# Attention and a two-layer network on one core: first weight kept in its loaded row order, heads renumbered, prologue reordered by unit of the hidden layer

## The chip, the core and the metric

The kernel runs on one core of a Trainium2 chip. The metric is device time in microseconds (us), from three timed runs; a profiled execution gives the time of every instruction. The core's engines run side by side, each in the order of its own instructions, and wait for each other by semaphores: TensorE (PE, matmuls; PEld are its weight loads), VectorE (DVE), ScalarE (ACT), GpSimd (POOL) and SyncE (SP, which here issues most DMAs). A matmul keeps one operand in the array (the weights, loaded beforehand, up to 128 x 128) and streams the other one, up to 512 columns. Results go to PSUM, eight banks of 512 float32 a partition; ACT and DVE move them to SBUF.

## The reference

There are B = 8 batches of H = 8 heads; a head has S = 512 rows of D = 64, and a state of NS = 32 rows. Each reads the other by softmax attention; the results, with heads side by side, are 544 rows of 512 a batch, and go through a layer norm and two weight matrices with a ReLU and a residual. The weights come as float64.

```python
scores = scale * x @ state.T                       # 512 x 32 a head
a = softmax(scores);   xread = a @ state           # 512 x 64
scores2 = scale * state @ x.T                      # 32 x 512
a2 = softmax(scores2); sread = a2 @ x              # 32 x 64
x = concat([xread, sread], rows), heads side by side   # 544 x 512 a batch
xn = (x - mean) / sqrt(var + 1e-6) * g_ln
out = x + relu(xn @ w_ch1) @ w_ch2                 # 512 x 2048, 2048 x 512
```

## The kernel before

The kernel keeps float32 accuracy with float16 matmuls: a value is split in a high and a low half, and a product is three matmuls (`TERMS`: high by high, high by low, low by high). As xread is a @ state, the first layer is a @ (state @ w1): **state products** (`state_products`, L662) multiply the states by w1 once a batch into `matrix`, and first products multiply `matrix` by the numerators `ea`. The hidden layer of 2048 is worked in U = 4 units of 512.

**Streams and the order.** Each function is a generator that yields single steps (one instruction, or a group of matmuls). `streams` (L930) lists them all, and `PLAN` (L40) is a written-out order: "17:3" issues step 3 of stream 17. `issue` (L191) only follows it, so each engine works off its steps in this order and waits where an operand or buffer isn't ready. `WARM` (L163) is the count of matmuls over constants, without use for the result, that the order puts between others.

**Prologue.** `attention(0)` (L346) works with `parts = 2`: 256 rows at a time. It finds the largest magnitudes, splits x and state (`x16`, `sh`), transposes them by DMA (`xT`, `sT`), takes scores (`scores`, L402), and softmax both ways. `weights1(u)` (L583) loads two halves of 1 MB of w1, makes float32 words of the float64 (`words`, L567: one ACT and two DVE instructions a half), subtracts the mean with matmuls in float32 (`means`, L599, and four DVE instructions), and finds a scale: ACT writes magnitudes, four matmuls over `ones` add them (`add`, L608), DVE takes the largest. Then `split` writes high and low halves, and four DMAs (L623) copy them into `w1c`, in which each 64-row head lies as high beside low. A state product is thus two passes over 128 rows, (high, high) and (low, low) of the state against (high, low) of the weight, for two groups of four heads: in each, four heads at once in column strips of 32:

```python
for a in range(2):
    for j in range(4):
        nc.tensor.matmul(ps[32 * j:32 * j + 32], lhsT=sT[:, g, a, 32 * j:32 * j + 32],
                         rhs=w[:, 2 * g + j // 2, j % 2], start=a == 0, stop=a == 1, ...)
```

`weights2(u)` (L625) does w2 alike; its scale comes from ACT with an accumulated sum and `across` (L324: a transpose, a reduction, a broadcast by matmul, a maximum). In the order before, all four `weights1` come first, then the state and first products of batch 0, then `weights2` and `second_products_by_unit` (L721). Sums and differences of w2's blocks (`sums_of_weights`, L743) serve the later batches' products with seven instead of eight block products. `common_scale` (L652) needs all units.

**A later batch.** `products(b)` (L774) runs, for two halves of the rows and four units, first products (L801), ReLU and sums on ACT, DVE and POOL, and 42 second products (L857); meanwhile the order has `attention(b + 1)` and `state_products(b + 1)` issued between them. There the state products take their results from the two PSUM banks `half`, which the first products use too, and scores, reads and mixes use the pair `banks` (a ring of one). **State reads** (`read_state`, L477): for each head and each quarter of the rows one matmul, with high and low half of x side by side as 128 weight columns and 64 columns streamed; ACT copies the result `z`, and `fold_halves` (L491) adds high and low with four float32 matmuls. Four small DMAs collect the reads of all batches in `sread_rows`; `state_rows` (L900) normalizes these 256 rows, and `products(8)` takes them through both layers (`first_of_state`, L806), with a copy of the weight's high halves in order of rows (`high_halves`, L893, eight DMAs).

## Time and profile before

| | |
|---|---|
| Timed runs | 666.25 us median of 3 (665.38 to 669.15) |
| Profiled execution, first to last instruction | 665.1 us |
| PE busy | 643.9 us in 6051 matmuls |
| DVE busy | 499.5 us in 1002 instructions |
| ACT busy | 388.8 us in 699 |
| POOL busy | 217.9 us in 189 |
| HBM read, written | 28.05 MB, 9.44 MB |
| Issue to landing of a 1 MB weight load | 8.2 to 8.6 us (median) |

The profile names an instruction by its line, engine, operation and "out<-in" with the program's tile names. Steps that go through `do` have the line of that helper, L188; matmul groups have the line of the matmul. A matmul's duration includes its way through the array, so matmuls that follow each other overlap; the distance from start to start shows what each costs in a stream. A tile shape such as 128*32 gives rows and columns of the weights.

### The profile page before, as it was taken

The page shows a single profiled execution, that of the slowest core. Times are in us where ns is not written, and L with a number is a line of the kernel's source. Part 1 is how long each engine was busy: PE and PEld are TensorE (multiplying, and loading weights), DVE is VectorE, ACT ScalarE, POOL GpSimd, SP SyncE. Part 2 cuts the span into 40 slices and gives each one's busy share as a digit, 9 for nine tenths or more (in the row PEclk, how much of TensorE's full clock was granted, in tenths as well). Part 3 has the DMA queues.
Part 4 walks back from the last instruction along what each step waited for, and adds up shares of the span by engine and source line. Part 5 has one row for each costly group of instructions (what it writes and reads, how often), then busy time and mean ns, then how long its engine had stood idle before and what let it go on. Part 6 is the DMA issues. An engine that isn't in the chain of part 4 may idle for free.

```text
span 665.1 us, 14886 instructions
## 1 busy us (share of the span) xinstructions
PE 643.9 (97%) x6051; PEld 499.6 (75%) x6051; DVE 499.5 (75%) x1002; ACT 388.8 (58%) x699; POOL 217.9 (33%) x189
## 2 busy tenths in 40 slices
PE   7997999999999999999999999999999999999996
PEld 2343655549887887788888888888778887888885
DVE  5998976687788677967887689777976897465533
ACT  5498889667546474547465656465546564344331
POOL 0000443321344315323452226333433343234222
PEclk8999999999999999999999999999999999999999
DMA  8999846825131434340416152405142411245211
GB/s 323 309 276 209 257 130 132 138 57 135 43 67 43 130 105 78 96 100 2 92 33 163 67 88 68 100 2 121 38 125 46 77 33 42 82 116 98 78 57 32
DMA packets 98564, 69.64 MB, mean 105 GB/s; under 512 B 72704, under 2 KB 90624, under 8 KB 98048
## 3 DMA queue, kind: packets, MB, share of 16 engines
q1 hardware_dynamic: 96384, 64.77, 38.4%
q0 software_dynamic: 864, 3.15, 2.5%
q8 instruction: 47, 0.77, 0.5%
q10 hardware_dynamic: 1248, 0.79, 0.4%
q14 instruction: 21, 0.17, 0.1%
HBM read 28.05 MB, written 9.44 MB: 56 GB/s over the span
## 4 chain that ended last, share of the span: by engine, by line
PE 86%; DVE 8%; DMA 3%; ACT 1%; issue 1%; SPq 0%; DVEq 0%
PE acc L857 41%; PE half L801 22%; PE acc L717 6%; PE half L667 5%; PE half L810 3%; DVE w_t L188 2%; PE acc L703 2%; PE acc L749 2%; PE banks L481 1%; PE banks L405 1%; PE banks L517 1%; DMA w1c<-raw 1%; DMA raw<-in_moe_w_ch_dram 1%; PE banks L494 1%; DMA x_f<-in_x_dram 1%
## 5 line engine op out<-in xcount | busy, mean ns | idle before, releaser
L857 PEld LDWEIGHTS <-xs 128*128 128x128 f16 x2520 | 242.4, 98 | 43.6 <-issue 15.3
L188 POOL TENSOR_TENSOR xs<-rs,xs 128x512 f16<-128x512 f32 x120 | 142.5, 1200 | 272.6 <-ACT xs L188 207.1
L857 PE MATMUL acc<-w2h,xs 128*128 128x256 f16 x1440 | 183.0, 273 | 0.0
L801 PE MATMUL half<-ea,matrix 128*128 128x256 f16 x1344 | 159.4, 273 | 0.0
L801 PEld LDWEIGHTS <-matrix 128*128 128x128 f16 x1344 | 130.7, 98 | 16.7 <-issue 0.8
L857 PE MATMUL acc<-sums,xs 128*128 128x256 f16 x1080 | 141.9, 273 | 0.0
L188 DVE SCALAR_TENSOR_TENSOR rs<-half,rs 128x256 f32<-128x256 f32 x224 | 89.4, 419 | 27.6 <-ACT rs L188 13.3
L188 ACT ACTIVATE xs<-rs 128x512 f16<-128x512 f32 x128 | 77.1, 618 | 40.5 <-DVE rs L188 33.8
L188 ACT ACTIVATE xs<-half 128x256 f16<-128x256 f32 (+1 forms) x112 | 53.7, 487 | 73.2 <-PE half L801 51.3
L188 DVE SCALAR_TENSOR_TENSOR xs<-half,xs 128x256 f16<-128x256 f32 (+1 forms) x112 | 61.2, 550 | 28.1 <-ACT xs L188 24.5
L188 ACT ACTIVATE matrix<-half,hs 128x512 f16<-128x512 f32 x56 | 38.1, 687 | 35.2 <-PE half L667 34.9
L188 DVE SCALAR_TENSOR_TENSOR matrix<-half,hs,matrix 128x512 f16<-128x512 f32 x56 | 41.2, 742 | 16.0 <-ACT matrix L188 15.3
L188 ACT ACTIVATE rs<-half 128x256 f32<-128x256 f32 x56 | 21.4, 382 | 42.4 <-PE half L801 40.0
L717 PE MATMUL acc<-w2h,hid 128*128 128x512 f16 x192 | 43.1, 379 | 0.0
L188 DVE TENSOR_TENSOR strip<-acc,strip 128x256 f32<-128x256 f32 (+1 forms) x60 | 33.2, 554 | 10.5 <-PE acc L857 7.5
L667 PE MATMUL half<-w1c,sT 128*32 128x512 f16 x448 | 33.5, 384 | 1.9 <-DVE rs L188 1.0
L717 PEld LDWEIGHTS <-hid 128*128 128x128 f16 x192 | 18.5, 98 | 20.9 <-issue 0.4
L188 POOL TENSOR_TENSOR ts<-ts,mA 128x1024 f32<-128x1024 f32 (+1 forms) x8 | 14.4, 1806 | 59.3 <-DVE mA L188 52.9
L188 PE MATMUL half<-ones 128*128 128x512 bf16 x103 | 28.0, 416 | 1.1 <-DVE ones L309 1.1
L188 DVE SCALAR_TENSOR_TENSOR x<-x_f,x_s,x 128x512 f16<-128x512 f32 x32 | 24.8, 799 | 5.3 <-ACT x L188 5.3
L188 POOL TENSOR_TENSOR hid<-strip,hid 128x512 f16<-128x512 f32 x16 | 19.5, 1232 | 26.9 <-ACT hid L188 26.8
L188 DVE BATCH_NORM_STATS2 s<-xr 128x6 f32<-128x512 f32 x32 | 21.6, 684 | 8.7 <-ACT xr L188 8.6
(154 smaller groups left out, 791.5 us busy)
## 6 DMA issues: line engine op xcount, KB each, us to landing
raw<-in_moe_w_ch_dram SPq DMA_DIRECT2D x9, 1024.0 KB, 8.6
out_dram<-xr SPq DMA_DIRECT2D x16, 512.0 KB, 3.7
x_f<-in_x_dram SPq DMA_DIRECT2D x15, 512.0 KB, 5.0
sums<-in_moe_w_ch_dram SPq DMA_DIRECT2D x7, 1024.0 KB, 8.2
ek<-ea SPq DMA_DIRECT2D x56, 64.0 KB, 2.0
ek<-ek SPq DMA_DIRECT2D x7, 512.0 KB, 4.3
xr<-part POOLq DMA_DIRECT2D x6, 512.0 KB, 5.0
w1c<-raw SPq DMA_DIRECT2D x8, 256.0 KB, 6.8
```

Of the source, the lines that this page charges most:

```text
L188: return lambda: f(*map(now, args), **{k: now(v) for k, v in kw.items()})
L405: nc.tensor.matmul(o[32 * j:32 * j + 32], lhsT=sT[:, g, a, 32 * j:32 * j + 32], rhs=xT[:, s, 4 * g + j].rearrange("p c t -> p (c t)"), sta ...
L481: nc.tensor.matmul(ps_z[:, h // 4, :, h % 4], lhsT=xv[:, c // hc, h, c % hc], rhs=ebT[:, :, h // 4, c, 32 * (h % 4):32 * (h % 4) + 32], st ...
L494: nc.tensor.matmul(pr[:, g], lhsT=z4[:, g, i], rhs=fold, start=i == 0, stop=i == 1, skip_group_check=True)
L517: nc.tensor.matmul(px[:, c, D * h:D * h + D], lhsT=ek[:, h // 4, h % 4, (2 * t + c) * P:(2 * t + c + 1) * P], rhs=sk[:, h], start=True, st ...
L667: nc.tensor.matmul(ps[32 * j:32 * j + 32], lhsT=sT[:, g, a, 32 * j:32 * j + 32], rhs=w[:, 2 * g + j // 2, j % 2], start=a == 0, stop=a == ...
L703: nc.tensor.matmul(o[:, 256 * f:256 * f + 256], lhsT=m[:, g, i, P * (q + f):P * (q + f) + P], rhs=ea[:, s, k, g], start=f == 0 and g == 0 ...
L717: nc.tensor.matmul(po, lhsT=hid[:, i, q, c * P:(c + 1) * P], rhs=w[:, j, q], start=first and q == 0 and n == 0, stop=last and q == 3 and n ...
L749: nc.tensor.matmul(o, lhsT=signs[:, k // 2], rhs=v[k], start=start and k == 0, stop=k == 3, skip_group_check=True)
L801: nc.tensor.matmul(ps[:, 256 * q:256 * q + 256], lhsT=m[:, h, i, P * (2 * k + q):P * (2 * k + q) + P], rhs=ea[:, 0, j, h, 256 * g:256 * g ...
L810: nc.tensor.matmul(ps[:, 256 * q:256 * q + 256].rearrange("p (t n) -> p t n", t=2), lhsT=w[:, k // 2, k % 2, fs] if k < H else wn[:, k - H ...
L857: nc.tensor.matmul(po[o], lhsT=y[:, n, i, o] if o < 2 else x[:, o - 2, n, i], rhs=v[j], start=u == 0 and n == 0 and k == 0 and o in (2, 1, ...
```

## The change

- `w1c` is no longer copied: `weights1` splits straight into it in the order of rows as loaded, with high and low halves as two blocks. Row d of an odd head lies in the upper 64 partitions. Head h = 2j + g goes to strip j of group g, where it was h = 4g + j; `state_of` finds its state, and batch 0 loads its state so.
- State products: three passes by `TERMS` over 64 rows each, both groups (row halves) and four heads (column strips) in one step of 24 matmuls. In batches from 1 on they write both banks of `banks`, and one ACT and one DVE instruction take both out.
- Scales: PE multiplies the upper 16 bits of the float32 words by themselves (`largest_square`: 16 matmuls of 128 x 128 a unit and weight), DVE takes the largest element, `across` follows, and the scale comes from its square root's exponent. The Abs passes and sums over `ones` go.
- State reads: 64 weight columns a matmul, two heads in two column strips, three of the four half products; DVE adds high and low, one PE transpose replaces `fold_halves`.
- Words are made in place (`t = raws[0]`), with other buffers.
- The streams of the prologue stand by unit: first weight, state products, first products, second weight, second products. The order (`PLAN`) is new throughout; `WARM` is 55, was 103. In the new order no warming matmul stands ahead of the first weight's `means`.
- The last stage uses the same weights without `high_halves`; its row transposes have eight blocks, had twelve.

```diff
+        if b > 0:
+            yield do(nc.sync.dma_start, out=sj, in_=state[b].rearrange("(g j) n d -> (j n) g d", g=G))
+        else:
+            for j in range(4):
+                yield do(nc.scalar.dma_start, out=sj[32 * j:32 * j + 32],
+                         in_=state[b, 2 * j:2 * j + 2].rearrange("g n d -> n g d"))
...
+    def scales_of_squares(m, s, inv, c):
+
+        yield do(nc.vector.tensor_scalar, inv.bitcast(I32), m.bitcast(I32), 1, HALF_EXP_MASK, ALU.logical_shift_right,
+                 ALU.bitwise_and)
+        yield do(nc.vector.tensor_scalar, inv, inv, 2.0**64 / c, None, ALU.mult)
+        yield do(nc.vector.reciprocal, s, inv)
...
+    def state_of(b, sT, g, j, a):
+
+        k, i = ((2 * j + g) // 4, (2 * j + g) % 4) if b > 0 else (g, j)
+        return sT[:, k, a, 32 * i:32 * i + 32]
...
-            for h in range(H):
+            for j in range(4):
                 for c in range(C):
-                    nc.tensor.matmul(ps_z[:, h // 4, :, h % 4], lhsT=xv[:, c // hc, h, c % hc],
-                                     rhs=ebT[:, :, h // 4, c, 32 * (h % 4):32 * (h % 4) + 32],
-                                     start=c == 0, stop=c == C - 1, skip_group_check=True)
+                    for i in range(2):
+                        for g in range(G):
+                            nc.tensor.matmul(ps_z[64 * g:64 * g + 64, j, 0:2 - i], lhsT=xv[:, c // hc, 2 * j + g, c % hc, i],
+                                             rhs=ebT[:, 0:2 - i, g, c, 32 * j:32 * j + 32],
+                                             start=c == 0 and i == 0, stop=c == C - 1, skip_group_check=True)
...
-        yield do(nc.scalar.activation, z, pz[:, 0], AF.Copy)
-
-        def fold_halves(pr, z4):
...
-        yield do(fold_halves, pr, z4)
+        yield do(nc.vector.tensor_reduce, z.rearrange("p (j n) -> p j n", j=4), ps_z.rearrange("p j i n -> p j n i"), AX.X,
+                 ALU.add)
+        yield do(nc.tensor.transpose, pz[:, 1, 0:P], z, idf)
...
+    def largest_square(t, total, m, top, col):
+
+        tops = t.bitcast(BF16).rearrange("p (e two) -> p e two", two=2)
+
+        def gram(v, ps, first, last):
+            for k in range(8):
+                c = v[:, 128 * k:128 * k + 128, 1]
+                nc.tensor.matmul(ps, lhsT=c, rhs=c, start=first and k == 0, stop=last and k == 7)
+        for h in range(2):
+            yield do(gram, tops[:, 1024 * h:1024 * h + 1024], total[:, 0:P], h == 0, h == 1)
+        yield do(nc.vector.tensor_reduce, col, total[:, 0:P], AX.X, ALU.max)
+        yield from across(col, 1, 1, m, top, total[:, P:3 * P])
...
+        yield from largest_square(t, accumulator(), m, of_weights[:, u, 3:4], of_weights[:, u, 1:2])
+        yield from scales_of_squares(m, scale, is1[:, u:u + 1], SW)
+        yield from split(w[:, 0], w[:, 1], t, scale)
+        w1c[u] = w.rearrange("p i (j f) -> p i j f", j=4)
...
+        def multiply(ps, sT, w):
+            for n, (i, k) in enumerate(TERMS):
                 for j in range(4):
-                    nc.tensor.matmul(ps[32 * j:32 * j + 32], lhsT=sT[:, g, a, 32 * j:32 * j + 32],
-                                     rhs=w[:, 2 * g + j // 2, j % 2], start=a == 0, stop=a == 1, skip_group_check=True)
+                    for g in range(G):
+                        r = slice(64 * g, 64 * g + 64)
+                        nc.tensor.matmul(ps[g][32 * j:32 * j + 32], lhsT=state_of(b, sT, g, j, i)[r], rhs=w[r, k, j],
+                                         start=n == 0, stop=n == 2, skip_group_check=True)
...
+                ps = banks()
+                scale = hs[:, u:u + 1]
+                yield do(lambda p, *a: multiply([p[:, g] for g in range(G)], *a), ps, sT, w1c[u])
+                yield do(nc.scalar.activation, m[:, :, 0], ps, AF.Copy, scale=scale)
+                yield do(nc.vector.scalar_tensor_tensor, m[:, :, 1], ps, scale, m[:, :, 0], ALU.mult, ALU.subtract)
...
-    streams = [gain(), attention(0), *map(weights1, range(U)), state_products(0), first_products(), *map(weights2, range(U)),
-               common_scale(), *map(second_products_by_unit, range(U)), attention(1), state_products(1),
-               *map(sums_of_weights, range(U))]
+    streams = [gain(), attention(0)]
+    for u in range(U):
+        streams += [weights1(u), state_products(0, (u,)), first_products(u), weights2(u), second_products_by_unit(u)]
+    streams += [common_scale(), attention(1), state_products(1), *map(sums_of_weights, range(U))]
```

More of the change, by code (lines that the diff above doesn't have):

```diff
@@ L30 @@
 S2 = 2.0**12
-CM = 2.0**-20
-SB = 2.0**15
+CM = 2.0**-24
+SB = 2.0**19
 SR = 2.0**-6
@@ L291, in load_batch @@
             yield do(engines[hh].dma_start, out=xf[:, hs], in_=src[:, hs])
-        yield do(nc.sync.dma_start, out=sj, in_=state[b].rearrange("(g j) n d -> (j n) g d", g=G))
+        if b > 0:
[4 more added lines that the diff above has]
+                         in_=state[b, 2 * j:2 * j + 2].rearrange("g n d -> n g d"))
         for r in range(4 if b > 0 else 0):
@@ L604, in weights1 @@
             yield do(nc.vector.scalar_tensor_tensor, t4[:, k], t4[:, k], gx[:, k:k + 1], ps, ALU.mult, ALU.subtract)
-        sizes = raws[0].bitcast(BF16)[:, 0:2048]
-        yield do(nc.scalar.activation, sizes, t, AF.Abs)
-        def add(total, v):
-            for k in range(4):
-                nc.tensor.matmul(total, lhsT=ones, rhs=v[:, 512 * k:512 * k + 512], start=k == 0, stop=k == 3)
-        yield do(add, total, sizes)
-        yield do(nc.vector.tensor_reduce, m, total, AX.X, ALU.max)
-        yield do(nc.vector.tensor_scalar_max, m, m, TINY)
-        yield from scales(m, scale, is1[:, u:u + 1])
-        hl = raws[1].bitcast(F16).rearrange("p (i e) -> p i e", i=2)
-        yield from split(hl[:, 0], hl[:, 1], t, scale)
-        hl = hl.rearrange("p i (k f) -> p i k f", k=4)
-        w = narrow(u, "w1c").bitcast(F16).rearrange("p (k s f) -> p k s f", k=4, s=2)
-        w1c[u] = w
-        for i in range(2):
-            for s in range(2):
-                to = 64 * (i ^ s)
-                yield do(nc.sync.dma_start, out=w[to:to + 64, :, s], in_=hl[64 * s:64 * s + 64, i])
+        yield from largest_square(t, accumulator(), m, of_weights[:, u, 3:4], of_weights[:, u, 1:2])
+        yield from scales_of_squares(m, scale, is1[:, u:u + 1], SW)
+        yield from split(w[:, 0], w[:, 1], t, scale)
+        w1c[u] = w.rearrange("p i (j f) -> p i j f", j=4)
     def weights2(u):
@@ L820, in block @@
                         else:
-                            yield do(first_of_state, ps, k, w1c[u], high[u], state_rows_T[0])
+                            yield do(first_of_state, ps, k, w1c[u], state_rows_T[0])
                             r = rs[:, 512 * k:512 * k + 512]
@@ L889, in products @@
             yield together()
-    high, state_rows_T = [None] * U, [None]
-    def high_halves(u):
-        high[u] = quad("high").bitcast(F16).rearrange("p (k f) -> p k f", k=4)
-        for s in range(2):
-            half = slice(64 * s, 64 * s + 64)
-            yield do(nc.sync.dma_start, out=high[u][half], in_=w1c[u][half, :, s])
+    state_rows_T = [None]
     def state_rows():
@@ L939, in moe_attention @@
         streams += these
-    streams += [list(state_rows()), *(list(high_halves(u)) for u in range(U))]
+    streams.append(list(state_rows()))
     streams += [list(s) for s in products(B)]
```

162 lines of the change are left out of this document (78 added, 84 removed), and 243 rows, old and new, of the table PLAN.

## The prediction

> **What bounds the kernel now.** I read the page first, for the busy shares and the chain.
>
> ```profile
> span 665.1 us, 14886 instructions
> PE 643.9 (97%) x6051; PEld 499.6 (75%) x6051; DVE 499.5 (75%) x1002; ACT 388.8 (58%) x699; POOL 217.9 (33%) x189
> PE 86%; DVE 8%; DMA 3%; ACT 1%; issue 1%; SPq 0%; DVEq 0%
> ```
>
> TensorE carries the chain. The table by stretches says where it does not. Its columns are length, then busy time and count of PE, PEld, DVE, ACT, POOL, then granted clock, DMA share and GB/s.
>
> ```profile
> 0.00:16.00 16.00, 11.42 (x36) 4.26 (x36) 8.86 (x23) 8.83 (x15) 0.70 (x6) 0.89 0.88 320
> 16.00:42.00 26.00, 23.37 (x111) 9.90 (x112) 25.64 (x46) 16.37 (x17) 0.00 (x0) 1.00 1.06 314
> 42.00:64.00 22.00, 17.67 (x185) 9.10 (x185) 19.93 (x29) 18.43 (x26) 2.10 (x2) 1.00 0.98 219
> 64.00:82.00 18.00, 15.97 (x166) 11.79 (x166) 17.17 (x33) 16.28 (x27) 6.55 (x5) 1.00 0.91 242
> 150.00:220.00 70.00, 70.00 (x730) 59.10 (x729) 54.51 (x120) 42.23 (x86) 24.56 (x20) 1.00 0.31 77
> ```
>
> From 150 us on PE is busy 70.00 of 70 us and DVE 78%: every PE nanosecond saved there should come off the time, if DVE keeps up. Between 16 and 82 us it is the other way round: DVE is busy 62.7 of 66 us (95%), while PE idles or runs matmuls that warm its clock. I followed both in the timeline of PE and DVE (start, length, what, count).
>
> ```profile
> 1.09 4.01 PE L188 MATMUL half<-ones 128*128 128x512 bf16 x9 [1.09 <-DVE ones L309]
> 6.26 0.69 DVE L188 TENSOR_REDUCE x_part<-x_f 128x1 f32<-128x512 f32 x1 [4.42 <-DMA x_f<-in_x_dram]
> 34.45 3.60 PE L601 MATMUL acc<-w_t,gm 128*128 128x512 f32 x8
> 41.16 0.68 DVE L188 SCALAR_TENSOR_TENSOR ea<-ef,ea 128x512 f16<-128x512 f32 x1
> 41.90 0.96 PE L532 MATMUL acc<-sh,ea 32*128 32x64 f16 x34 [0.50 <-DVE ea L188]
> 57.91 1.05 PE L667 MATMUL acc<-w1c,sT 128*32 128x512 f16 x16 [3.50 <-DMA w1c<-raw]
> 63.94 1.48 PE L703 MATMUL acc<-ea,matrix 128*128 128x256 f16 x12
> 79.37 1.05 PE L667 MATMUL acc<-w1c,sT 128*32 128x512 f16 x16
> 80.35 2.79 PE L703 MATMUL acc<-ea,matrix 128*128 128x256 f16 x24
> 147.65 1.47 PE L749 MATMUL acc<-w2h,signs 128*128 128x256 f16 x12
> 149.05 0.62 PE L667 MATMUL half<-w1c,sT 128*32 128x512 f16 x8
> 149.60 1.48 PE L801 MATMUL half<-ea,matrix 128*128 128x256 f16 x12
> 156.60 1.10 PE L481 MATMUL banks<-ebT,x 128*128 128x64 f16 x32
> 157.53 1.47 PE L801 MATMUL half<-ea,matrix 128*128 128x256 f16 x12
> 158.84 1.00 PE L494 MATMUL banks<-fold,z 128*128 128x64 f32 x8
> 159.68 0.38 PE L749 MATMUL acc<-w2h,signs 128*128 128x256 f16 x2
> 164.11 0.82 PE L857 MATMUL acc<-sums,xs 128*128 128x256 f16 x6
> 657.19 2.13 PE L857 MATMUL acc<-w2h,xs 128*128 128x256 f16 x18
> ```
>
> Batch 0's numerators `ea` begin to be ready at 41 us, but its first products start at 63.94: the state products before them stood behind the copies into `w1c` (3.50 us of wait) and behind other units' weights. The group rows (busy, mean of one, idle before), and one row of the DMA issues (size, us to landing), give the rest.
>
> ```profile
> L188 PE MATMUL half<-ones 128*128 128x512 bf16 x103 | 28.0, 416 | 1.1 <-DVE ones L309 1.1
> L667 PE MATMUL half<-w1c,sT 128*32 128x512 f16 x448 | 33.5, 384 | 1.9 <-DVE rs L188 1.0 <-DVE xs L188 0.9
> L717 PE MATMUL acc<-w2h,hid 128*128 128x512 f16 x192 | 43.1, 379 | 0.0
> L601 PE MATMUL acc<-w_t,gm 128*128 128x512 f32 x32 | 14.6, 598 | 0.6 <-DVE w_t L188 0.5
> L610 PE MATMUL acc<-raw,ones 128*128 128x512 bf16 x12 | 3.1, 379 | 1.7 <-ACT raw L188 1.7
> L188 ACT ACTIVATE matrix<-half,hs 128x512 f16<-128x512 f32 x56 | 38.1, 687 | 35.2 <-PE half L667 34.9
> L188 DVE SCALAR_TENSOR_TENSOR matrix<-half,hs,matrix 128x512 f16<-128x512 f32 x56 | 41.2, 742 | 16.0 <-ACT matrix L188 15.3
> L188 ACT ACTIVATE xr<-banks,ux 128x1024 f32<-128x1024 f32 x14 | 15.6, 1112 | 6.0 <-PE banks L517 5.3 <-DMA s_r<-in_state_dram 0.5
> L188 DVE SCALAR_TENSOR_TENSOR eb<-eB,eb 128x1024 f16<-128x1024 f32 x8 | 10.5, 1310 | 1.3 <-ACT eb L188 1.3
> L188 DVE TENSOR_SCALAR raw<-raw 128x1024 uint32<-128x1024 uint32 x9 | 6.2, 694 | 0.6 <-DMA raw<-in_moe_w_ch_dram 0.5
> L188 DVE SCALAR_TENSOR_TENSOR w_t<-raw 128x1024 uint32<-128x1024 uint32 x7 | 8.5, 1221 | 0.0
> L188 DVE SCALAR_TENSOR_TENSOR w_t<-w_t,gx,acc 128x512 f32<-128x512 f32 x16 | 11.0, 742 | 0.0
> L188 DVE SCALAR_TENSOR_TENSOR raw<-w_t,of_weights,raw 128x2048 f16<-128x2048 f32 x2 | 4.6, 2346 | 0.0
> raw<-in_moe_w_ch_dram SPq DMA_DIRECT2D x9, 1024.0 KB, 8.6
> ```
>
> The mean of a matmul holds its latency; what it costs in a dense stream is the step from start to start: 1.31 us for twelve of 256 columns (157.53 to 158.84), 0.109 each; 512 columns take twice that, 0.22. The 103 warming matmuls thus hold 22 us.
>
> **State products.** Now a unit is two visits of eight 32-column matmuls, four column strips at once. Eight take 0.55 us (149.05 to 149.60), sixteen 0.98 (79.37 to 80.35): a pass of four is (0.98 - 0.55)/2 = 0.215, and 0.12 is leaving the strip shape. Entering costs 0.09: the twelve matmuls at 147.65 should end their stream after 1.31, and the next starts after 1.40. So a visit is 0.64, and the 448/8 = 56 visits of batches 1 to 7 are 35.8 us, some 34 where two stand together. After: 28 visits of 24 matmuls. If the two 64-row halves run at once, as the four column strips do, a visit is 3 x 0.215 + 0.21 = 0.855, in all 23.9: **10.1 us saved**, 1.45 of it for batch 1 in the prologue, and another 1.1 in batch 0. If the halves don't overlap it is 6 x 0.215 + 0.21 = 1.50 a unit, 8 us lost. I take the overlap: the 34 matmuls at 41.90 use 32-row strips of 128 columns, and where the order passes from one row strip to the next they run into each other: (0.96 - 0.19)/33 = 23 ns apart, against (1.10 - 0.19)/31 = 29 for the full-height ones of the same width at 156.60 (0.19 is one's length, 1.10 being 31 x 0.029 and a last one).
>
> The results move from a ring of two `half` banks to the single pair `banks`, which attention uses too. One ACT instruction of 1.11 and one DVE of 1.31 replace two of 0.69 and two of 0.74, so both engines do less. A use holds the pair 0.86 + 1.11 + 1.31 = 3.3 us; four a batch, and attention's own (some 14 us), fill 27 of the 66 us of a batch ((659 - 164)/7.5, the state rows counting half). I cost it at nothing, covered by the first and second products, which are nearly all of a batch; where the order puts two close together, PE waits 2.4 us with those products queued behind it.
>
> **State reads.** Before: 32 matmuls in 0.93 us and the fold in 0.84 (158.84 to 159.68), 1.78 a batch. After: 64 matmuls of 64 weight columns in two column strips. Lower bound: each strip streams 16 of 64 and 16 of 32 columns, 0.72 to 0.93 us. Upper bound with the strips loading side by side: the fold's float32 matmuls come every 0.84/8 = 0.105 us though 64 columns of float32 should stream in about 0.055 (512 take (3.60 - 0.60)/7 = 0.43 in the stream at 34.45), so the loading of 128 weight columns sets that step, half of it for 64: 32 x 0.053 = 1.7. I take 1.3, between them. With 0.2 for changing shape and 0.25 for the transpose that replaces the fold: 1.75, **no gain**; the bounds are -0.6 and +0.4 a batch, -5 and +3 us over eight. ACT's copy of z becomes a DVE reduction of 0.4 us a batch, under the 22% that DVE has free.
>
> The Trainium skill (TensorEngine Tiling (Array Packing), Restrictions) says that column tiling rules out the fast weight load; by the estimate of a weight column per 1/1.2 ns in TensorE: Matmul & The Clock Gate, LDWEIGHTS, 64 columns are 53 ns and the read 1.7 us, 3 us more in the sum than mine. It agrees with the bound from the fold's rows; no row shows a 64-column strip.
>
> **Scales.** The sixteen sums over `ones` (16 x 0.216 = 3.5 us, twelve of them in the L610 row) and the Abs passes of ACT go; 128 matmuls of 128 columns come, between 0.055 (half of 0.109) and 0.105 (the fold's step) each, 7 to 13.4; I take 7, the moving side being what a 16-bit row shows. Four more rounds of `across` at some 0.37 add 1.5. Together **+5 us** of PE, in the prologue, up to +11.
>
> **Prologue by unit.** Before, PE works off the prologue without stops from 82 us, and second products of batch 1 begin at 164.11. When can batch 0's first products begin after? DVE decides. Ahead of the `ea` write at 41.16 the old order has 38 us of DVE by the group means, and took 34.9 from the arrival of x at 6.26, 0.91 of it. Ahead of the last write of unit 0's matrix the new order has 39: 35 instructions of attention (18.6); the unit's first weight, 2 x (0.69 + 1.22) for the words, 4 x 0.74, 2.35 and 1.2 of small ones (10.3); the words of its second weight and small ones (5.1); the words of the next unit (3.9); the rest small. So 6.3 + 0.91 x 39.7 + about 1.7, because without warming at the start the first means run at half clock for some us (the nine warming matmuls at 1.09 are (4.01 - 0.4)/8 = 0.45 us apart, twice the warm step, and cost 2 us by that): **44.5 us against 63.94**. But PE has done less by then. Before: means 32 x 0.43 = 13.7, sums 3.5, state products, scores, mix, read 7.7, together 24.9. After: half of the means 6.9, grams 1.8, the rest 5.6, together 14.3. From 63.94 to 164.11 PE had 100.2 - 4.5 (idle and warming, 2.0 of it in the row from 64 to 82) = 95.7 us of work. After: 95.7 + 10.6 + 2.4 (the +5 above, less 1.1 and 1.45 of state products) = 108.7, so 153.2 and what PE waits, x. From unit 0's first products to unit 1's second ones the new order asks DVE for 58 x 0.91 = 53 us by the same means and PE for 48.5, so x is 4 to 5 there; from then on DVE has 49 for PE's 64. x lies between 0 and 13 (what PE idled or warmed from 42 to 64 us before); I take 5. **158 against 164, 6 us saved**, from -2 to +11. The 48 warming matmuls that go (10 us) are inside this: what they covered is in the 44.5. The removed copies into `w1c` (16) and `high` (8) free SP's queue and end the 3.50 us wait; next late is the split itself. The loads of w2's first unit now pass ahead of w1's others on SP; at 8.6 us to landing they are there long before DVE wants them.
>
> **Tail.** The state rows keep 2 x 12 matmuls a unit and half, and the last 6.1 us (span less 659) stay.
>
> Sum: 665.1 - 6 (prologue, with the shares of batches 0 and 1) - 8.7 (state products of batches 2 to 7) + 0 (reads) = 650.4 of span; the profiled execution lasted 665.1 from first to last instruction, and the median of the runs is 1.1 above that: **651.5 us**.
>
> **Rivals.** *No overlap of row halves* (slower): the two 64-row halves of a state product follow each other, 1.50 us a unit: +8 in batches 1 to 7 and +0.8 in batch 0 in place of -10.1 and -1.1, so 651.5 + 20 = 671.5. It decides from 1.21 us a unit on (34/28), above which state products cost more than before. The 23 ns between row strips speak against it; for it, that no row shows halves of 64 rows together with column strips. *Loads in the way*: the two column strips of the read share one path for weights, so 64 loads of 0.053 follow each other, 3.4 us a read and 3.85 with transpose and change of shape, 2.1 more than before in each of eight batches: 651.5 + 17 = 668.5, a little above the old time and hard to tell from it. Against it: the 32-column strips at 149.05 load four weights per 0.215 unseen; for it: there is 0.215 to hide them, and here 0.03. *PE waits all through the prologue, or behind `banks`*: DVE and ACT as full as from 16 to 82 us before, x = 13 and a few stops later: 660 to 666. *Everything fits*: x near 0 and reads at their lower bound: 642.
>
> **How the numbers follow.** Forecast, 645 to 660: 0.62. Better: 0.10. Waits, 660 to 666: 0.14. Loads: 0.05. Row halves: 0.05; an order that puts waits of both kinds into every batch, over 670: 0.04. A measurement tells about 0.5%, 3.3 us, from no change, so faster ends at 662.9: 0.62 + 0.10 + 0.05 of the waits = 0.77; the same, the other 0.09 and the loads, 0.14; slower 0.09. The range 642 to 664 leaves out the slow cases, the worst of the waits and the best tail.
>
> **What would show it.** State products as visits of 24, next work 0.75 us after their start; 1.1 to 1.7 us for the 64 reads; first products of batch 0 at 43 to 46; second products of batch 1 at 153 to 164; PE at 70 of 70 after. Wrong if a visit takes 1.4 us, a read over 2.5, or PE stands before `banks` in every batch.

## The result, and the profile after

The changed kernel takes 703.87 us (median of 4 runs, 702.4 to 705.23) where the kernel before takes 665.82 (665.33 to 669.15): ratio 1.056, 95% interval 1.053 to 1.0589. The forecast was 651.5, in a range of 642 to 664. The profiled execution spans 701.2 us, 36.1 more than before's.

First the page after, its first line and the busy times:

```profile
span 701.2 us, 15843 instructions
PE 636.5 (91%) x6583; PEld 498.4 (71%) x6583; DVE 513.8 (73%) x998; ACT 359.9 (51%) x651; POOL 229.8 (33%) x189
```

TensorE has 7.4 us less to do than before (643.9) and is busy 91% instead of 97%: the work went, and waits came. VectorE is busy 14 us longer with four instructions fewer. The table by stretches shows where TensorE stands (columns as in the prediction):

```profile
220.00:290.00 70.00, 63.96 (x768) 52.11 (x769) 58.80 (x111) 38.38 (x71) 25.74 (x20) 1.00 0.38 93
290.00:360.00 70.00, 60.16 (x612) 48.31 (x610) 49.61 (x94) 34.57 (x65) 23.64 (x20) 0.95 0.35 88
...
570.00:640.00 70.00, 69.71 (x779) 60.02 (x780) 43.72 (x87) 29.97 (x54) 25.70 (x22) 1.00 0.16 48
```

Before, the stretch from 150 to 220 us had 70.00 of 70. The timeline of TensorE answers to the rows on which the costs of the parts were built:

```profile
54.21 0.71 PE L724 MATMUL acc<-ea,matrix 128*128 128x256 f16 x5
...
129.42 1.19 PE L504 MATMUL banks<-ebT,x 128*64 128x64 f16 x64
130.54 2.76 PE L738 MATMUL acc<-w2h,hid 128*128 128x512 f16 x12
...
139.03 0.84 PE L683 MATMUL banks<-w1c,sT 64*32 64x512 f16 x24
139.80 0.61 PE L770 MATMUL acc<-w2h,signs 128*128 128x256 f16 x4
...
176.88 1.36 PE L880 MATMUL acc<-w2h,xs 128*128 128x256 f16 x11
```

A state product is a visit of 0.77 us from start to start, a read 1.12: both as cheap as hoped, or cheaper. But the first products start at 54.21 instead of the forecast 44.5, and batch 1's second products at 176.88, 12.8 us later than before (164.11) where 6 us earlier was forecast. From there to the end it is 524.3 us against 501.0, another 23.3. The waits of TensorE from 176 us on (in all, how often, the longest):

```profile
PE half L822 <- DVE rs L189: 5.8, 2, 4.1
PE banks L504 <- DMA ebT<-eb: 3.3, 1, 3.3
PE banks L534 <- DMA ek<-ek: 3.2, 3, 2.1
PE acc L880 <- DVE xs L189: 3.0, 2, 2.2
PE acc L880 <- POOL xs L189: 2.9, 3, 1.5
PE half L822 <- DVE xs L189: 2.9, 2, 2.7
```

With the shorter ones its idle time there is 28.1 us; before it was 1.9. None of the long ones is a wait until the shared pair of banks comes free, which I had named as the danger (such waits are 1.3 us in all): TensorE waits for VectorE, GpSimd and the DMAs instead. Two places show how. The start, VectorE first, then ScalarE's queue:

```profile
11.49 0.28 DVE L189 TENSOR_REDUCE x_am<-s_j 128x1 f32<-128x128 f32 x1 [4.90 <-DMA s_j<-in_state_dram]
...
17.35 0.17 DVE L189 TENSOR_SCALAR gm<-gx 128x4 f32<-128x4 f32 x1 [3.79 <-DMA gx<-in_moe_g_ln_dram]
17.43 0.15 DVE L189 TENSOR_SCALAR x_m<-banks 128x2 f32<-128x2 f32 x1
```

```profile
1.26 4.96 ACTq L189 DMA_DIRECT2D s_j<-in_state_dram  x4
9.31 0.39 ACTq L309 DMA_DIRECT2D gx<-in_moe_g_ln_dram  x1
9.73 1.28 ACT L327 ACT_TABLE_LOAD   x1 [9.73 <-DMA sums<-in_moe_w_ch_dram]
```

The issuing itself is short: the four small loads of the state take 2.1 of their 4.96 us. But the fourth, the ninth load of the two queues together, waits for a semaphore that an earlier load raises, and leaves at 5.90, when an x load has landed (5.88). The gain's load waits in the same way for the first weight load (9.29) and leaves at 9.31; that is the release which the last row names. VectorE, for which the order puts `gm` ahead of `x_m`, stands 8.7 us behind the two. And the longest wait of the steady stretch, at 350 us:

```profile
349.25 1.91 POOL L189 TENSOR_TENSOR ts<-ts,mA 128x1024 f32<-128x1024 f32 x1 [4.30 <-DMA sread_rows<-sread]
349.42 2.82 DVE L189 SCALAR_TENSOR_TENSOR eb<-eB,eb 128x1024 f16<-128x1024 f32 x1
...
352.57 0.68 DVE L189 SCALAR_TENSOR_TENSOR xs<-half,xs 128x512 f16<-128x512 f32 x1
...
353.17 0.86 DVE L189 SCALAR_TENSOR_TENSOR rs<-half,rs 128x256 f32<-128x256 f32 x2
...
354.09 1.25 PE L822 MATMUL half<-ea,matrix 128*128 128x256 f16 x5 [4.11 <-DVE rs L189]
```

The split of `eb`, 1.31 us on average before, takes 2.82 here, ending 1.1 us after the GpSimd instruction on `ts` beside it, and what TensorE needs is queued behind it. (That the one makes the other long is shown by pool_light below.) Then the clock drops as well; the same stretch in steps of 2 us (the last three columns are clock, DMA share, GB/s):

```profile
352.00:354.00 2.00, 0.00 (x0) 0.00 (x0) 1.97 (x7) 0.73 (x2) 0.73 (x1) 0.64 0.27 55
354.00:356.00 2.00, 1.91 (x10) 1.35 (x11) 1.93 (x5) 0.76 (x2) 1.63 (x2) 0.50 1.11 207
356.00:358.00 2.00, 2.00 (x11) 1.44 (x10) 1.15 (x3) 0.87 (x2) 2.00 (x2) 0.50 0.01 1
...
360.00:362.00 2.00, 2.00 (x73) 1.86 (x73) 2.00 (x4) 0.63 (x1) 0.87 (x1) 1.00 0.00 0
```

The sum of the 23.3 us, in time from start to start: +26.2 waits; +6.4 because the first and second products run slower (427.2 us against 420.8, and twelve fewer of them); -6.9 state products; -3.1 reads with fold or transpose; +1 at the end; -0.4 small ones. The clock explains about 4.4 of the 6.4 (an estimate: 8.8 us of work fall into the stretches at half clock, at 352.6 to 359.4 and 492.5 to 495.9).

### The profile page after: what moved, and what is told of

The parts are those of the page before. It is cut to its first block, busy times and chain, and to the rows that moved or that the text cites. A ratio compares the mean times of both kernels' runs of the same rounds, so it can differ in the third digit from the quotient of the medians.

```text
span 701.2 us, 15843 instructions
## 1 busy us (share of the span) xinstructions
PE 636.5 (91%) x6583; PEld 498.4 (71%) x6583; DVE 513.8 (73%) x998; ACT 359.9 (51%) x651; POOL 229.8 (33%) x189
## 5 line engine op out<-in xcount | busy, mean ns | idle before, releaser
L189 POOL TENSOR_TENSOR xs<-rs,xs 128x512 f16<-128x512 f32 x120 | 147.6, 1240 | 309.6 <-ACT xs L189 231.3
L822 PE MATMUL half<-ea,matrix 128*128 128x256 f16 x1344 | 162.7, 275 | 10.5 <-DVE rs L189 5.8
L189 ACT ACTIVATE xs<-rs 128x512 f16<-128x512 f32 (+1 forms) x128 | 76.7, 618 | 51.3 <-DVE rs L189 46.4
L189 DVE SCALAR_TENSOR_TENSOR matrix<-banks,hs,matrix 128x1024 f16<-128x1024 f32 x28 | 35.8, 1277 | 17.4 <-ACT matrix L189 17.4
L189 ACT ACTIVATE matrix<-banks,hs 128x1024 f16<-128x1024 f32 x28 | 31.1, 1111 | 11.8 <-PE banks L683 10.4
L189 POOL TENSOR_TENSOR hid<-strip,hid 128x512 f16<-128x512 f32 x16 | 26.2, 1652 | 21.8 <-ACT hid L189 19.1
L189 DVE SCALAR_TENSOR_TENSOR x<-x_f,x_s,x 128x512 f16<-128x512 f32 x32 | 30.1, 971 | 3.2 <-ACT x L189 3.2
L189 ACT ACTIVATE x<-x_f,x_s 128x512 f16<-128x512 f32 x32 | 21.7, 712 | 8.4 <-DVE x_s L189 6.2
L189 DVE SCALAR_TENSOR_TENSOR xr<-strip,of_second,xr 128x512 f32<-128x512 f32 x28 | 24.2, 876 | 2.1 <-POOL strip L189 1.8
```

Of the source, the lines that this page charges most:

```text
L189: return lambda: f(*map(now, args), **{k: now(v) for k, v in kw.items()})
L822: nc.tensor.matmul(ps[:, 256 * q:256 * q + 256], lhsT=m[:, h, i, P * (2 * k + q):P * (2 * k + q) + P], rhs=ea[:, 0, j, h, 256 * g:256 * g ...
```

## The experiments

Theory 1: the new written-out order alone makes the waits. Theory 2: the shared pair of banks makes them, in any order. Theory 3: the prologue is late because of the loads at the start. Theory 4, added later: VectorE is late because of GpSimd. All kernels with their one profiled execution; "start" is when batch 1's second products begin, "rest" the span behind it, "idle" TensorE's idle time in the rest up to its last matmul. The kernel before took 666.9 to 667.4 us (medians) beside them. Most times are of one run; the five of p1w_start_warm and p1w_again, one kernel, lie 6 us apart, so smaller differences between single runs say little.

| kernel | time | span | start | rest | idle |
|---|---|---|---|---|---|
| before | 665.82 | 665.1 | 164.11 | 501.0 | 1.9 |
| after | 703.87 | 701.2 | 176.88 | 524.3 | 28.1 |
| e1_old_order | 720.73 | 718.9 | 174.39 | 544.5 | 43.1 |
| rev_new_order | 707.40 | 705.6 | 178.34 | 527.3 | 21.9 |
| bo_banks_old_order | 723.19 | 721.4 | 178.04 | 543.4 | 37.0 |
| bo2_pair_only | 710.39 | 708.6 | 163.28 | 545.3 | 36.3 |
| e1h_halves | 686.07 | 684.3 | 175.41 | 508.9 | 5.2 |
| pool_light | 685.44 | 683.5 | 174.98 | 508.5 | 15.9 |
| p1_start | 697.12 | 695.3 | 169.65 | 525.7 | 27.7 |
| p1w_start_warm | 700.60 | 697.8 | 167.92 | 529.9 | 29.5 |
| p1w_again (median of 4) | 696.83 | 696.0 | 167.27 | 528.7 | 28.2 |
| r1_vector_first | 695.86 | 694.0 | 167.94 | 526.1 | 27.7 |
| e1m_pairs_where_free | 676.54 | 674.5 | 166.07 | 508.4 | 8.6 |
| e2p_pairs_by_time | 691.48 | 689.7 | 167.34 | 522.4 | 28.8 |
| rd_reads_only | 664.32 | 663.2 | 163.94 | 499.3 | 3.4 |
| rd2_reads_mended | 662.25 | 661.8 | 164.51 | 497.3 | 1.3 |

### Old order, new order, and the pair

**e1_old_order.** The edit in short; the order itself is a string of 2609 steps, not printed here.

```diff
-issue(tc, streams, PLAN)
+issue(tc, streams, PLAN_AFTER[to 30:0] + PLAN_BEFORE[the rest, renumbered])
```

> The changed kernel's operations, buffers and prologue, but from the first instruction of batch 2's loads on (right after step 30:0 of the written-out order) the order of the kernel before, step for step; only the state products' steps stand a few places earlier or later, where the shared pair of PSUM banks is free, and the scores stand behind both transposes of xT. Theory 1 (the new written-out order makes VectorE, GpSimd and the DMAs late for TensorE): the waits of TensorE behind 176 us fall from 28 us to under 6, and with the prologue's 12.8 us still there the time is 665 us (655 to 675). Theory 2 (state products in the one pair of banks, with evacuations of 128x1024, force the waits in any order): 700 us (690 to 710), with waits of 20 us and more behind 176 us.

Measured 720.73: 17 us slower than the changed kernel. Theory 1, in which the new order alone makes the waits, falls. The waits of TensorE in it, the first lines:

```profile
PE banks L684 <- DVE matrix L190: 16.3, 8, 3.9
PE banks L535 <- DVE matrix L190: 7.3, 4, 2.6
...
PE banks L428 <- DVE matrix L190: 4.2, 1, 4.2
```

All three stand before the shared pair (L684 state products, L535 mix, L428 scores), until VectorE has taken the last matrix out of it.

**rev_new_order** and **bo_banks_old_order**, the other half of the exchange.

```diff
-            for g in range(G):
-                ps = accumulator() if b == 0 else half()
...
+            if b > 1:
+                ps, scale = banks(), hs[:, u:u + 1]
+                yield do(both, ps, sT, w1c[u])
+                yield do(nc.scalar.activation, m[:, :, 0], ps, AF.Copy, scale=scale)
+                yield do(nc.vector.scalar_tensor_tensor, m[:, :, 1], ps, scale, m[:, :, 0], ALU.mult, ALU.subtract)
```

With that edit both take the state products through the pair; rev has the new order behind the prologue, and bo the old one with the pairs at the places of e1_old_order.

> The other half of the exchange: the kernel before with its own operations and prologue, state products of batches 2 to 7 evacuated as pairs through the shared banks (16 matmuls, one ScalarE and one VectorE instruction over both banks), and behind the prologue the new written-out order, up to the state rows. Theory 1: the order brings its waits with it, 20 to 30 us of them, and the time is 680 to 697 us where the kernel before takes 666. Theory 2: what is lost is lost to the shared banks, so this kernel and the one with the old order and the same banks (bo_banks_old_order) take the same time, both 680 to 690 us. If the column-tiled reads, the scales or the three passes are what the order cannot cover, both stay at 666.

> The kernel before in its own order, with one part of the change alone: state products of batches 2 to 7 as pairs through the shared banks, three steps a unit instead of six, at the places where e1_old_order has them. Theory 1: 666 us, between 660 and 671. Theory 2: 680 us or more, with TensorE waiting for the banks.

rev took 707.40, its rest 26.3 us more than before's: with before's own operations and the pair, the new order has most of the changed kernel's waits (21.9 us idle), the longest ones at the same places and of the same size. Its waits for VectorE at the head of the list:

```profile
PE half L813 <- DVE rs L191: 5.7, 2, 4.1
PE half L813 <- DVE xs L191: 3.6, 4, 2.7
```

So reads, scales and passes are not what makes them. bo took 723.19, with TensorE waiting for the pair as in e1_old_order, but it had part of the prologue in another order, which cost it a wait of 3.9 us at 161; bo2 does without.

**bo2_pair_only**: the edit of bo, the rest of the order exactly before's.

> The kernel before, step for step in its own order, with the state products of batches 2 to 7 alone made as pairs in the shared banks (its own 16 matmuls a unit, one ScalarE and one VectorE instruction of 128x1024), each at the place nearest to the old one at which the pair is free in the written order. In bo_banks_old_order the stretch from 83 to 170 us was in another order than before's as well and held 5 us of waits of its own; here it is not. Theory 2 (the pair is what the old order cannot hold): about 712 us (705 to 718), with waits of 25 us and more in which TensorE waits for VectorE's evacuation of a matrix. Theory 1 (only the new order is at fault): 666 us (662 to 672).

710.39. The one thing that I had costed at nothing costs 44 us here, alone:

```profile
PE banks L667 <- DVE matrix L188: 15.8, 8, 3.7
PE banks L517 <- DVE matrix L188: 6.6, 4, 2.5
PE banks L405 <- DVE matrix L188: 4.8, 1, 4.8
```

**e1h_halves.**

```diff
-                ps = banks()
-                yield do(lambda p, *a: multiply([p[:, g] for g in range(G)], *a), ps, sT, w1c[u])
+                for g in range(G):
+                    ps = half()
+                    yield do(lambda p, *a, g=g: multiply([p], *a, only=g), ps, sT, w1c[u])
```

> e1_old_order with one thing undone: the state products of batches 2 to 7 go through the single banks again, two visits a unit, six steps, at the places where the kernel before has them; the three passes, the column-tiled reads, the scales and the prologue stay as changed. Each visit is 12 matmuls on one half of the rows, so the two halves no longer overlap: two visits of about 0.75 us instead of one of 0.77, some 17 us of TensorE time more than e1_old_order over 24 units. If the shared pair makes the waits: they fall from 40 us to under 8 and the time is 683 us (676 to 690) in spite of the 17 us. If the new operations do not fit the old order for another reason (reads, scales, VectorE's reduce in place of ScalarE's copy), the waits stay and the time is 725 us or more.

686.07: 35 us less than e1_old_order, although its state products take TensorE longer (34.8 us from start to start for the 576 matmuls of batches 2 to 7, 20.0 in e1_old_order). Idle time 5.2 instead of 43.1; the group of the state products has hardly any:

```profile
L686 PE MATMUL half<-w1c,sT 64*32 64x512 f16 x576 | 37.8, 379 | 1.9 <-DVE rs L192 1.0 <-DVE xs L192 0.9
```

The old order carries every new operation almost without waits except the pair. That is shown; what it leaves open is whether the pair or my places for it are to blame.

**e1m_pairs_where_free** and **e2p_pairs_by_time** (8 and all 24 units in PAIRS; both with the mended start of p1w below).

```diff
-            if b > 1:
+            if b > 1 and (b, u) not in PAIRS:
                 scale = hs[:, u:u + 1]
```

> e1h_halves with the start of p1w_start_warm, and 8 of the 24 units of state products of batches 2 to 7 made as pairs again: those 8 for which the old order, added up with the durations of the traces, leaves the shared banks unused from 0.8 us before the visit to 6.3 us after it (for the other 16 no such place lies between the matrix's last use and its next). Per pair 0.73 us of TensorE time less than two visits. If the pair costs only where the banks are wanted again: 686 - 7 - 2.6 - 6 = 670.5 us (667 to 674), with no wait by a matrix of over 0.5 us. If a pair costs wherever it stands (longer evacuations on ScalarE and VectorE): 678 us or more.

> e1m_pairs_where_free with all 24 units of batches 2 to 7 as pairs, each at the place that, by the durations of the traces added up along the old order, leaves the most time between the pair's neighbours in the shared banks; at 13 of the 24 the time is short, by 0.4 to 2.5 us, 17.6 us in all. The start is the mended one. Against e1m the other 16 pairs give 16 x 0.73 = 12 us of TensorE. If the waits are the shortfalls and no more: 676.5 - 12 + 17.6 = 682 us (677 to 687), and most of what e1_old_order lost (720.7, or 711 with the mended start) was my choice of places. If the pair costs 40 us in the old order wherever it is put: 705 us or more. If the shortfalls are hidden: 665 to 672.

e1m: 676.54, between the two expectations. Taking the start of p1w (175.41 - 166.07 = 9.3 us) off e1h gives 676.7, so eight pairs gave nothing: 5.0 us of state products less, 3.4 us of idle time more, hardly any of it before the pair:

```profile
PE acc L890 <- POOL xs L192: 3.8, 4, 1.4
PE banks L192 <- DVE z L192: 1.5, 1, 1.5
...
PE banks L686 <- DVE ts L192: 0.5, 1, 0.5
```

e2p: 691.48, between its expectations again. Better places save 22 us (rest 522.4 against 544.5), so half of what e1_old_order lost was my choice. With the other half, the rest is still 14 us longer than with eight pairs, though the state products take 10 us less. Its first waits stand before the pair again:

```profile
PE banks L685 <- DVE matrix L191: 6.0, 5, 2.2
PE banks L685 <- ACT eB L191: 4.5, 3, 2.2
```

In the old order the pair makes the waits, and how many depends on its places. For the new order this half is not shown: it was never run with the state products in the single banks, so whether it would wait without the pair stays open.

**pool_light.**

```diff
-                        yield do(nc.gpsimd.tensor_tensor, x[:, 1 + 2 * k:3 + 2 * k, :, 1], s[:, 2 * k:2 * k + 2],
-                                 x[:, 1 + 2 * k:3 + 2 * k, :, 0], ALU.subtract)
+                        yield do(nc.gpsimd.memset, x[:, 1 + 2 * k:3 + 2 * k, :, 1], 0.0)
...
-            yield do(engine.tensor_tensor, t3, t3, m_.unsqueeze(2).broadcast_to([P, NK, 32]), ALU.subtract)
+            few = NK if engine is nc.vector else 4
+            yield do(engine.tensor_tensor, t3[:, 0:few], t3[:, 0:few], m_[:, 0:few].unsqueeze(2).broadcast_to([P, few, 32]), ALU.subtract)
```

> The changed kernel with its order, in which GpSimd's work behind the prologue is cut: the low halves of the sums (xs) are set to zero instead of computed, and the subtraction and the product of the softmax over the state are done on 128 of 1024 columns. That part of the computation is left out. Theory 4 (VectorE is late because its instructions from SBUF to SBUF stand until the GpSimd instruction beside them ends, 799 ns becoming up to 1683 for the same split of x): the means of those groups return to those of the kernel before or below, VectorE's busy time falls by 15 us or more, the waits by VectorE of 2.7, 2.2 and 4.1 us at 218, 331 and 350 us go or fall under 1 us, and the time is 680 us (674 to 688). If VectorE is late only for its place in the queue, it stays at 695 to 701.

This kernel leaves out most of GpSimd's work, so it computes something else, and only its times are read. 685.44, at the upper end of the expectation. The groups of VectorE, after and then here:

```profile
L189 DVE SCALAR_TENSOR_TENSOR rs<-half,rs 128x256 f32<-128x256 f32 x224 | 90.7, 416 | 37.1 <-ACT rs L189 18.8 <-ACT xs L189 10.8 <-PE half L822 4.2
L189 DVE SCALAR_TENSOR_TENSOR x<-x_f,x_s,x 128x512 f16<-128x512 f32 x32 | 30.1, 971 | 3.2 <-ACT x L189 3.2
L189 DVE SCALAR_TENSOR_TENSOR eb<-eB,eb 128x1024 f16<-128x1024 f32 x8 | 14.7, 1842 | 0.8 <-ACT eb L189 0.8
```

```profile
L189 DVE SCALAR_TENSOR_TENSOR rs<-half,rs 128x256 f32<-128x256 f32 x224 | 91.7, 423 | 42.9 <-ACT rs L189 21.0 <-ACT xs L189 12.7 <-PE half L823 5.8
L189 DVE SCALAR_TENSOR_TENSOR x<-x_f,x_s,x 128x512 f16<-128x512 f32 x32 | 24.7, 802 | 3.8 <-ACT x L189 3.8
L189 DVE SCALAR_TENSOR_TENSOR eb<-eB,eb 128x1024 f16<-128x1024 f32 x8 | 10.8, 1349 | 0.8 <-ACT eb L189 0.8
```

The splits from SBUF return nearly to the means that they had before (799 and 1310); the instructions that read PSUM hardly changed. It is the new order that puts the two engines' instructions side by side: the split of `eb` has a mean of 1828 in rev_new_order and 1346 in e1_old_order. VectorE's busy time falls by 28 us, idle time from 28.1 to 15.9. Theory 4 carries about half of the new order's waits; GpSimd's own lateness (2.9 us in the list of after) is in that half too, since this kernel leaves out that work too. The other half stays, and its cause is open.

**r1_vector_first.**

```diff
-    "87:44 78:10 78:7 78:9"
+    "78:10 78:7 78:9 87:44"
```

That is the place at 342 us, one of seven, without the steps between (a dozen steps move in all); 87:44 is the split of `eb`, 78 the products.

> p1w_start_warm with 20 or so steps of the written-out order moved by some places: at six waits of p1_start (211, 289, 323, 342, 415, 558 us) the VectorE steps of the products that TensorE waits for go ahead of the attention's VectorE steps (splits of x, eb and the maxima), and at 482 us the read of the state goes behind the next first product. Nothing else changes. If VectorE's place in the queue makes those waits: 2.7, 2.2, 4.1, 0.7, 1.7 and 3.3 us go or shrink to a quarter, with some 5 us of halved clock behind the two longest, and the time is 680 us (674 to 686). If GpSimd's instructions beside VectorE's make them, or the work is only pushed to the next wait, it stays within 4 us of p1w_start_warm.

695.86, 4.7 us less than p1w_start_warm's single run and 1.0 less than its median. The waits that I aimed at are gone or smaller, and others stand in their place:

```profile
PE half L828 <- DVE xs L195: 4.3, 2, 4.1
PE acc L886 <- ACT xs L195: 3.8, 2, 2.1
PE acc L886 <- POOL xs L195: 3.7, 4, 1.7
```

Idle time is 27.7 us, as in p1_start. Moving these few steps of VectorE's queue did not shorten the waits in all; they came back at other places.

### The start

**p1_start.**

```diff
-    drain(load_batch(0, first_tiles))
     gx = tiny("gx", C)
     nc.scalar.dma_start(out=gx, in_=g_ln.rearrange("(j p) -> p j", p=P))
+    drain(load_batch(0, first_tiles))
...
-                yield do(nc.scalar.dma_start, out=sj[32 * j:32 * j + 32],
+                yield do(nc.sync.dma_start, out=sj[32 * j:32 * j + 32],
```

> The changed kernel with its whole order, and only two things of the start put differently: the gain's small load is issued first on ScalarE's queue, and the four loads of s_j go to SyncE's queue instead of ScalarE's. Theory 3 (the prologue is late because ScalarE issues six loads one after the other, and VectorE stands behind s_j and the gain): the first products of batch 0 start near 46 us instead of 54.2, second products of batch 1 near 169 instead of 176.9, and the time falls by about 8 us, to 693 (690 to 697). If the prologue is set by the weights' loads and their scales instead, the first products move but the second products of batch 1 stay at 175 to 177, and so does the time, 701.

697.12. No load of ScalarE's queue waits for another now, and VectorE no longer stands for the gain (`x_m` at 10.39 instead of 17.43); first products start at 47.01, second products at 169.65:

```profile
7.68 0.29 DVE L189 TENSOR_REDUCE x_am<-s_j 128x1 f32<-128x128 f32 x1 [1.92 <-DMA s_j<-in_state_dram]
...
9.58 0.15 DVE L189 TENSOR_SCALAR gm<-gx 128x4 f32<-128x4 f32 x1
```

The 7.2 us by which both points come earlier are Theory 3, shown for the two edits together; 6.8 us come off the time. Still, the prologue by unit is 5.5 us later than the old one, not 6 earlier.

**p1w_start_warm** and **p1w_again** (the same kernel).

```diff
-WARM = 55
+WARM = 67
-    "1:15"
+    "1:15 177:55-66"
```

> p1_start with 12 more warming matmuls ahead of the first means, in the 5.0 us in which TensorE stood idle there (10.35 to 15.35 us). In p1_start the first eight means took 6.4 us where the kernel before has 3.7. If the cold clock is what they cost: 3.7 us for the eight, and the time falls from 697 to 694.4 us (693.5 to 695.5). If VectorE sets the pace of the prologue anyway, the means are shorter and the time stays at 696.5 to 697.5.

> p1w_start_warm once more, timed in rounds. Its prologue was 1.7 us shorter than p1_start's as expected, its time 3.5 us longer, with waits for transposes and copies of 1 to 2 us at 260, 279 and 292 us that p1_start did not have. If those waits belong to one execution: 695 us, like p1_start or below. If the shifted start makes them: 699 us or more in every run.

The first eight means, p1_start and then p1w_start_warm:

```profile
15.35 6.43 PE L632 MATMUL acc<-sums,gm 128*128 128x512 f32 x8 [4.99 <-DVE sums L189]
```

```profile
15.27 3.92 PE L638 MATMUL acc<-sums,gm 128*128 128x512 f32 x8 [0.80 <-DVE sums L195]
```

2.5 us shorter, as expected, and second products 1.7 us earlier. The time was 700.60 in the first run and 694.53 to 699.67 (median 696.83) in the four others, 1.0451 of before (1.0404 to 1.0498): the 1.7 us are lost among times that differ by 5 us from run to run. Whether warming helps the total is left open.

### One part alone, and a faster kernel

**rd_reads_only.**

```diff
-                    nc.tensor.matmul(ps_z[:, h // 4, :, h % 4], lhsT=xv[:, c // hc, h, c % hc],
-                                     rhs=ebT[:, :, h // 4, c, 32 * (h % 4):32 * (h % 4) + 32],
+                            nc.tensor.matmul(ps_z[64 * g:64 * g + 64, j, 0:2 - i], lhsT=xv[:, c // hc, 4 * g + j, c % hc, i],
+                                             rhs=ebT[:, 0:2 - i, g, c, 32 * j:32 * j + 32],
...
-        yield do(nc.scalar.activation, z, pz[:, 0], AF.Copy)
+        yield do(nc.vector.tensor_reduce, z.rearrange("p (j n) -> p j n", j=4), ps_z.rearrange("p j i n -> p j n i"), AX.X, ALU.add)
```

> The kernel before with the column-tiled state reads alone (64 matmuls in place of 32 of twice the width, one VectorE reduce of 128x256 in place of ScalarE's copy of 128x512, one transpose in place of four fold matmuls), the order untouched. The changed kernel's trace has 1.12 us for the 64 matmuls and 0.33 for the transpose against 1.78 in all that was forecast for before's: by that 8 batches give about 3 us, 662.5 us (660 to 665). Rival: the reduce stands in VectorE's queue, which is 75% busy, and the wait for it takes the gain back, 666 us or more.

664.32 (median of 8), ratio 0.9963 (0.9946 to 0.9981): a gain of 2.5 us, as expected, with three waits of 3.4 us in all left in it.

**rd2_reads_mended.**

```diff
-    "61:44 61:45 56:10 56:9 56:4"
+    "56:10 56:9 56:4 61:44 61:45"
...
-    "81:46 81:57"
+    "81:57 81:46"
...
-    "121:35 116:4"
+    "116:4 121:35"
```

The order is that of the kernel before, without the steps between; 61, 81 and 121 are attention, 56 and 116 products.

> rd_reads_only with its three waits of TensorE (0.96 us at 272, 1.50 at 359, 0.92 at 471) met by moving three VectorE steps: the split of eb and its transpose behind the products' splits, the read's reduce ahead of the reciprocal, the split of sk behind the products' split. If each was only a matter of the place in VectorE's queue: 3 us less than rd_reads_only, 661.3 us (660 to 663). If they come back elsewhere: 664.

662.25 (median of 5), ratio 0.9922 (0.9908 to 0.9936): 0.8% faster than the kernel before. One wait is left in the list from 164 us on:

```profile
PE banks L515 <- DMA ek<-ek: 1.3, 1, 1.3
```

Four moved steps sufficed here where a dozen did nothing in r1_vector_first. That this order had slack to move into, and the new one had not, is my reading, not shown.

## Why the prediction was wrong, by its own steps

From the forecast span of 650.4 us to the measured 701.2 it is 50.8 us. 18.9 of them lie ahead of batch 1's second products (158 forecast, 176.88 measured), 31.9 behind.

**State products.** Right: forecast 0.855 us a visit, measured 0.77 to the next work; the row halves overlap, and the first rival falls.

**The shared pair.** "I cost it at nothing, covered by the first and second products" is a step that failed: it took the share of time in which the pair is held (27 of 66 us) for the question. A use was to hold the pair for 3.3 us; in the changed kernel it holds it for 3.3 to 8.9, 4.7 on average, because ScalarE and VectorE come to it late. What seems to decide is whether, between a matrix's last use and its next, there is a stretch long enough between the attention's uses; by my adding-up, the old order had one for 8 of 24 units, and the 8 pairs put there made hardly any such waits (e1m). In the old order the pair alone cost 44 us with my first places (bo2); with the best that I found, going from 8 pairs to 24 still made 20 us of idle time (e2p against e1m). In the new order TensorE hardly waits before the pair, and yet the rest is 23 us longer than before's. "An order that puts waits of both kinds into every batch", over 670, was in my chances, at 0.04; the time came out there, but the waits were mostly not those before the pair.

**The order.** This is the step that failed by the most in the changed kernel. I costed the parts and took the new order of all steps as harmless in the steady stretch ("PE at 70 of 70 after"), so its waits stood in the sum at nothing. They came to 26.2 us more than before, with 6.4 us of slower products behind them. The condition that I had set, "if DVE keeps up", was not met at the places where VectorE's work came late. About 12 us of the idle time hang on GpSimd's instructions, which the new order puts beside VectorE's (pool_light). For the other half, in which TensorE also waits for VectorE and the DMAs, the cause stays open, and with it the share that the pair has in it. The order was the largest edit in the diff, and no view of the profile of before could show it; it should have widened the range upward.

**Reads.** Forecast no gain, bounds -5 and +3. The size was off, towards the lower bound: 64 matmuls take 1.12 us and not 1.3, and the part alone gives 2.5 us, with its waits mended 5 (0.78%). The loads are not in the way, so that rival falls. The Trainium skill says that column tiling rules out the fast weight load (TensorEngine Tiling (Array Packing), Restrictions); the estimate of 53 ns a load that I drew from it and from TensorE: Matmul & The Clock Gate, LDWEIGHTS, does not show in the trace, where a matmul with its load takes 1.12/64 = 17.5 ns.

**Scales.** A term slightly mis-sized: the 128 new matmuls take 8.5 us from start to start, where I took 7 (eight alone 0.61, from 30.13 to 30.74; sixteen together 0.92, from 84.52 to 85.44).

**Prologue.** First products: forecast 44.5, measured 54.21. The step that failed is "6.3 + ...": it took VectorE's start from the arrival of x and left out the loads of `s_j` and the gain that the diff puts on ScalarE's queue, where they wait until earlier loads have landed. With them mended they start at 47.01, and with a warm start as well at 44.42. That this last is the forecast's number is luck: the forecast counted 1.7 us for the cold start (2.5 measured), and its terms add up to 44.1, not 44.5. From first to second products I reckoned 108.7 us of work and 5 of waits; it was 116.0 and 6.7. So x was about right, and the work 7.3 us short. 1.3 us of that I had taken off the old prologue too much (idle and warming are 3.0 us there and not 4.5, work 97.0), 1.6 are twelve first products of batch 1 that the new order puts ahead of this point (72 against 60), and 1.0 the scales. The rest I did not trace.

**Tail.** 6.1 us forecast (5.8 in the trace of before), 6.8 measured from the last matmul to the end.

## What to carry to other kernels

When a change moves results into a buffer that others use, lay out the other uses along the time axis and look for the gap that each new use needs; the share of time in use says little. A written-out order is a part of the kernel with a price of its own: test a new part alone in the old order first, as the reads show, which gave 0.8% by themselves while the whole change lost 5.6%. And count the loads that an edit puts at the start: in these kernels the ninth leaves only when an earlier one has landed, and a whole engine may stand behind it.

## What the runs showed of the hardware

- VectorE's instructions with two SBUF operands stand while a GpSimd instruction that started first runs beside them: a split that takes 0.75 us elsewhere took 2.18 beside a GpSimd instruction of 1.91 (in rd_reads_only, at 469 us). With most of GpSimd's work left out (pool_light), the mean of the splits of x fell from 971 to 802 ns; instructions that read PSUM kept theirs (416 and 423). The Trainium skill (SBUF — State Buffer, Who interferes with whom) says so: a VectorE instruction with two SBUF inputs contends with a GpSimd instruction that reads SBUF, and the order of issue decides which one blocks. The trace agrees.
- The granted clock falls to 0.50 for 3.4 us or a few times that. Around the wait of 4.1 us at 350 it was 0.50 from 352.6 to 359.4; the 5.3 us of work in that stretch took twice as long, so the wait cost some 2.7 us more than itself (an estimate). A wait of 2.7 us left it at 1.00 in the changed kernel (at 218) and brought it to 0.50 from 212.8 to 216.2 in p1w_again, where TensorE was busy for 1.3 of the 3.4 us ahead of the drop; in p1w_start_warm a wait of 1.6 us was enough (at 89, busy 1.8 of 3.4). The Trainium skill (TensorE: Matmul & The Clock Gate, What's actually happening) puts the drop to half rate behind an idle window of about 3.4 us. The traces agree on the length of the window, but TensorE did not have to be idle for all of it.
